# Pooled attention into a gated expert layer on one core: wider loads, block-by-block conversion of W's first half, and another order of the first loads

## The chip, the cores and the metric

One core of a Trainium2 chip runs the whole program. The metric is the device time of one execution in microseconds (us); for the kernel before it is 782.62 us, the median of three runs (781.56 to 783.02). The core's engines are called by the names of the profile: PE (matrix multiplies, with PEld for its weight loads), DVE (vector), ACT (scalar and activation functions), POOL (GpSimd) and SP (it only issues transfers here). Each engine works through its own list of instructions in the order in which the program emits them.

## The reference

```
q, k, v: 8 batches x 8 heads x 576 tokens x 64, float32
k_p, v_p = mean over groups of 8 tokens          # 72 pooled keys and values per head
scores   = q @ k_p^T / 8;  attn = softmax(scores)
x        = attn @ v_p, heads side by side        # 4608 tokens x 512
a, b     = x @ w1, x @ w2                        # 512 -> 1024 each
out      = ((a * b) @ w3) @ w_out                # 1024 -> 1024 -> 512, float32
```

The four weight matrices come as 64-bit floats, q, k and v as 32-bit ones.

## The kernel before, in words

There is nothing nonlinear between `w3` and `w_out`, so the kernel first forms W = w3 @ w_out (1024 x 512) and then needs only two products per token: into a and b, and with W. All products are done in three passes over a high and a low part of each operand (`PASSES`, high*high, high*low, low*high), which `split` (line 157) makes: ACT casts the high part, DVE subtracts it to get the low part.

**The first stage makes W's first half** (rows 0 to 511), in eight blocks `s` = 0 to 7. For each block two loads of 512 KB come in, `load_w3` (line 118) and `load_wo` (line 114). Each is a block of 64-bit floats that must be turned into 32-bit ones: `high` (line 131, ACT) takes the upper word, `low` (line 138, DVE) or `low_act` (line 143, ACT) takes bits of the lower word, and `conv_b` (line 152, DVE) joins them. The w3 block is then turned on PE by four transposes (`w_turn`, line 213), and both blocks are split. `w_block` (line 170) does this in three stages of a pipeline: its call `v` converts block v, turns and casts block v-1 and subtracts the low part of block v-2's second operand. `w_mm` (line 629) then adds 12 matrix products of 512 columns into four PSUM banks. So the turn of block 1 stands ahead of the products of block 0 on PE.

**The second stage makes W's second half** (s = 8 to 15), with `w_conv`, `w_conv2` and `w_split` (lines 220 to 227); the second operand stays in SBUF from the first stage. Beside it runs the attention of the first chunk of 384 tokens: keys of batch 0 are loaded (`load_k`, line 316: four loads, each with 72 partitions), summed in groups of eight (`prep_k`, line 325, on POOL by a tree of three adds, or on DVE by one reduction where `K_DVE` says so), transposed (`kt_mm`, line 335, four transposes of 72 columns into one PSUM bank) and scaled; queries are loaded (`load_q3`, line 292), transposed on PE and copied; then come scores, softmax (`soft1` to `soft3`, with the exponentials on ACT), the transposes of the probabilities and the product with the pooled values. The 72 keys of a head don't fit 128 partitions evenly for two heads, so 16 of the 144 rows of a pair of heads are handled apart: `load_vr` (line 360) loads them four times over, with a broadcast as the outermost dimension of the source.

**The third stage is the first chunk of the main loop** (m = 0): per block j of 128 hidden units `a_mm`, `b_mm` (12 products each) and, two steps later, `out_mm` (9 products), while the attention of the second chunk and the conversions of w1 and w2 (`load_w12`, line 125, `w12_conv`) run beside it. After it come ten more chunks in a steady loop and a short last piece.

**The order of the work is written by hand.** `at(kind, k, fn, ...)` (line 648) puts a step on a plan; the plan is sorted (line 777) by the whole part of k, then by kind (L loads, P work on DVE, ACT and POOL, with the turns of W, M matrix products, A products of the attention), then by the fraction of k. `F0` = 4, `K0` = 20 and `M0` = 36 are the steps at which the three stages begin. The order in which a step is emitted is the order in which every engine, SP among them, takes it up. A tile in SBUF or PSUM that has a limited number of buffers makes a load or a matrix product wait until an older user has let go: the raw w3 blocks use four cells in turn (`raw_cell(s % 4)`), keys and values four buffers (`st_tile`), attention's PSUM tiles (`patt`) three, and w1 and w2 go to cells in the order `FREED` (line 106), as W's products and conversions release them. SP waits at such a load, and every load behind it waits too.

`warm` (line 207) issues transposes that nobody reads, 36 at the very start and 12 before the first products of W.

## Time and profile before

| | before |
|---|---|
| median of 3 runs | 782.62 us (781.56 to 783.02) |
| profiled execution, its own time | 782.46 us |
| its span in the profile, first to last instruction | 780.7 us |
| PE busy | 756.3 us, 97% of the span |
| DVE, ACT, POOL busy | 60%, 37%, 25% |
| bytes read from and written to memory | 52.43 and 9.44 MB |

The span leaves 1.76 us of the execution's own time outside. The views used below are: the page (busy time by engine), the table by stage (busy time of each engine in a stretch of time, with the granted clock of PE as a share, the mean busy share of the 16 transfer engines and the rate of the transfers), the waits (who waited for whom, in total, how often, the longest), the timeline (start, length, engine, line, operation, out<-in, with the idle time ahead of it and what ended it in brackets) and the chain of work that ended last (start, length, engine, tile and line). "x12" is a count of instructions merged into one line. PE's records overlap, because products are pipelined: a group's pace is read from the starts of its neighbours.

### The profile page before, as it was taken

To read this page: it belongs to the slowest core of one execution; us is meant where nothing else is said; L and a number is where in the kernel's file an instruction comes from. 1 tells how busy PE (TensorE), PEld (TensorE's weight loads), DVE (VectorE), ACT (ScalarE), POOL (GpSimd) and SP (SyncE) were. 2 spreads that over 40 slices of the span, in tenths; PEclk is the share of its full clock that TensorE was granted. 3 is DMA by queue.
4 is the path that set the end of the run, shared out by engine and by line. 5 is a ranking of instruction groups with operands and counts; after the bars stand their busy time and mean duration, and the time that the engine had idled before them with its cause. 6 is when DMAs were issued, how large, how long until landed. Compare 5 with 4: busy or idle time off the path is not lost.

```text
span 780.7 us, 11495 instructions
## 1 busy us (share of the span) xinstructions
PE 756.3 (97%) x4146; PEld 699.9 (90%) x4146; DVE 468.1 (60%) x923; ACT 287.7 (37%) x710; POOL 195.2 (25%) x234
## 2 busy tenths in 40 slices
PE   8978989999999999999999999999999999999998
PEld 7767877999999998999999998999999989999997
DVE  6866887475484476485574576575574675662212
ACT  5567977332233333232233333322332332332211
POOL 2334565105208202006117202025035220000000
PEclk9999999999999999999999999999999999999999
DMA  9999970026245233037044323136154222120101
GB/s 329 280 210 212 271 169 15 1 78 126 55 116 107 62 99 66 7 111 146 23 122 87 94 69 61 41 89 128 41 134 96 70 68 46 53 50 1 40 1 41
DMA packets 123913, 74.43 MB, mean 95 GB/s; under 512 B 75600, under 2 KB 107600, under 8 KB 123856
## 3 DMA queue, kind: packets, MB, share of 16 engines
q1 hardware_dynamic: 123856, 73.69, 38.4%
q8 instruction: 33, 0.54, 0.3%
q14 instruction: 24, 0.20, 0.1%
HBM read 52.43 MB, written 9.44 MB: 79 GB/s over the span
## 4 chain that ended last, share of the span: by engine, by line
PE 76%; DVE 10%; DMA 5%; ACT 4%; SPq 2%; issue 1%; POOL 0%; POOLq 0%; DVEq 0%; ACTq 0%
PE o L609 22%; PE a L574 21%; PE b L574 21%; DMA raw<-in_moe_w_dram 4%; PE att L415 3%; PE o L635 2%; DVE T L498 2%; DMA st<-in_v_dram 1%; DVE E L453 1%; PE att L549 1%; PE att L551 1%; PE att L550 1%; PE att L548 1%; DVE E L433 1%; DVE mx L431 1%
## 5 line engine op out<-in xcount | busy, mean ns | idle before, releaser
L574 PE MATMUL a<-xT,hl 128*128 128x384 f32 x1152 | 221.0, 339 | 0.4 <-POOL hl L159 0.4
L574 PE MATMUL b<-xT,hl 128*128 128x384 f32 x1152 | 220.9, 339 | 0.0
L574 PEld LDWEIGHTS a<-xT,hl 128*128 128x128 f32 x1152 | 201.1, 188 | 5.4 <-POOL hl L159 0.7
L574 PEld LDWEIGHTS b<-xT,hl 128*128 128x128 f32 x1152 | 199.7, 188 | 0.0
L609 PE MATMUL o<-Wc,gh 128*128 128x512 f32 x576 | 180.6, 395 | 0.0
L373 POOL TENSOR_TENSOR st<-st 72x512 f32<-72x512 f32 (+1 forms) x53 | 71.8, 1354 | 225.6 <-DMA st<-in_k_dram 170.3
L609 PEld LDWEIGHTS o<-Wc,gh 128*128 128x128 f32 x576 | 106.7, 188 | 17.1
L594 DVE TENSOR_TENSOR a<-b,a 128x384 f32<-128x384 f32 x96 | 52.8, 550 | 111.5 <-PE b L574 111.5
L609 PE MATMUL o<-Wc,gl 128*128 128x512 f32 x288 | 114.3, 397 | 3.3 <-DVE gl L600 3.3
L595 ACT CAST gh<-a 128x384 fp32r<-128x384 f32 x96 | 49.3, 513 | 151.9 <-DVE a L594 151.9
L584 ACT COPY a<-a 128x384 f32<-128x384 f32 x96 | 45.9, 479 | 110.5 <-PE a L574 86.6
L436 ACT ACTIVATE E<-E 128x288 f32<-128x288 f32 (+1 forms) x70 | 31.1, 445 | 118.3 <-DVE E L433 118.3
L600 DVE TENSOR_TENSOR gl<-a,gh 128x384 fp32r<-128x384 f32 x96 | 63.6, 663 | 13.6 <-ACT gh L595 13.6
L609 PEld LDWEIGHTS o<-Wc,gl 128*128 128x128 f32 x288 | 54.1, 188 | 17.1 <-DVE gl L600 4.6
L560 DVE TENSOR_TENSOR xT<-att,xT 128x384 fp32r<-128x384 f32 x48 | 26.5, 555 | 60.7 <-ACT xT L559 60.7
L386 POOL TENSOR_TENSOR vbd<-vm,vbd 64x256 fp32r<-64x256 f32 x16 | 12.5, 781 | 183.7 <-ACT vbd L385 183.4
L415 PE MATMUL att<-kbd,qT 128*128 128x144 f32 (+1 forms) x320 | 52.3, 286 | 2.4 <-DVE PTx L532 2.2
L415 PEld LDWEIGHTS att<-kbd,qT 128*128 128x128 f32 (+1 forms) x320 | 47.2, 178 | 6.9 <-DVE PTx L532 2.9
L437 DVE TENSOR_REDUCE sm<-E 128x4 f32<-128x288 f32 (+1 forms) x70 | 31.6, 451 | 35.8 <-ACT E L436 35.8
L159 DVE TENSOR_TENSOR PTx<-PTx,PTh 128x512 fp32r<-128x512 f32 (+1 forms) x33 | 27.7, 838 | 35.0 <-ACT PTh L158 32.8
L374 POOL TENSOR_TENSOR st<-st 72x256 f32<-72x256 f32 (+1 forms) x53 | 44.5, 840 | 4.2
L431 DVE TENSOR_REDUCE mx<-att 128x4 f32<-128x288 f32 (+1 forms) x80 | 35.2, 440 | 14.9 <-PE att L415 14.9
(93 smaller groups left out, 802.5 us busy)
## 6 DMA issues: line engine op xcount, KB each, us to landing
raw<-in_moe_w_dram SPq DMA_DIRECT2D x32, 512.0 KB
PTx<-T SPq DMA_DIRECT2D x120, 96.0 KB
st<-in_k_dram SPq DMA_DIRECT2D x32, 288.0 KB
out_dram<-ob SPq DMA_DIRECT2D x35, 256.0 KB
st<-in_v_dram SPq DMA_DIRECT2D x32, 256.0 KB
qs<-in_q_dram SPq DMA_DIRECT2D x128, 48.0 KB
raw<-in_moe_w_out_dram SPq DMA_DIRECT2D x8, 512.0 KB
st<-in_v_dram SPq DMA_DIRECT2D x64, 64.0 KB
```

Of the source, the lines that this page charges most:

```text
L373: nc.gpsimd.tensor_tensor(out=t[:, :, 0:4], in0=t[:, :, 0:4], in1=t[:, :, 4:8], op=ALU.add)
L374: nc.gpsimd.tensor_tensor(out=t[:, :, 0:2], in0=t[:, :, 0:2], in1=t[:, :, 2:4], op=ALU.add)
L415: nc.tensor.matmul(out=ps[:nt, 2 * KP * j:2 * KP * (j + 1)], lhsT=qT[n][:, pr, off:off + nt], rhs=kbd[b % 2][:, pr], start=True, stop=True,)
L431: nc.vector.tensor_reduce(out=mx[:nt, hs], in_=sv, axis=AX.X, op=ALU.min)
L436: nc.scalar.activation(out=E[:nt, hs], in_=E[:nt, hs], func=AF.Exp, scale=-1.0)
L437: nc.vector.reduce_sum(out=sm[:nt, hs], in_=E[:nt, hs], axis=AX.X)
L574: nc.tensor.matmul(out=o, lhsT=w12[j, w][sw][:, kt * P:(kt + 1) * P], rhs=x[sx][:, kt], start=(i == 0), stop=(i == 3 * NK - 1))
L584: nc.scalar.copy(out=a, in_=gt[m, j][:, :CH])
L594: nc.vector.tensor_tensor(out=g, in0=ps[:, :CH], in1=g, op=ALU.mult)
L595: nc.scalar.copy(out=gh, in_=g)
L600: nc.vector.tensor_tensor(out=gl, in0=g, in1=f(gh), op=ALU.subtract)
L609: nc.tensor.matmul(out=oacc[m][t], lhsT=(gh, gl)[sg][:, c], rhs=W[j][sw], start=(j == 0 and i == 0), stop=(j == NJ - 1 and i == 2))
```

## The change

It does these things:

1. **Wide loads.** `load_k` takes the 576 pooled-key groups of a batch as rows of one list, 256 rows to a load on 128 partitions (two rows each) and a last load of 64: three loads for four. `load_v` takes 128 consecutive groups of a pair of heads in one load on 128 partitions: two for four. `load_vr` joins neighbouring rows, with the rows outermost and the broadcast inside: six loads for eight. `load_q3` loads two heads at once: four for eight in the first chunk, eight for sixteen in the second. The layouts that follow from it: sums of keys are written twice side by side (`dup`), so that one transpose gives both halves of the partitions, and `kt_mm` has six transposes in two PSUM tiles instead of four in one, `kt_post` four scalings instead of two. `K_DVE` keeps DVE reductions for the last load of 64 rows of batches 0 and 1 alone. The parts of `soft3` and `prep_vr` use the matching order.
2. **W's first half block by block.** `w_block(s)` converts block s, `w_block2(s)` turns and splits it, and then its products follow; no other block's turn stands ahead of them. For five of the eight blocks the lower word of the second operand is taken on ACT (`low_act`), not on DVE. In the first half the three passes run over both tiles together, with high*low last.
3. **Another order of the first loads.** All loads of W's first half go first, then w3's block 8, the keys and the queries of the first chunk, w3's blocks 9 and 10, the values, w3's block 11, the rows apart, and then the rest of w3.
4. **Second half converted later.** `w_conv`, `w_conv2` and `w_split` stand 2.5, 1.9 and 1 steps ahead of the products instead of 7, 6 and 1.5. The transposes of the first chunk's queries move from steps 17, 18, 19 and 20 to 19, 19, 20 and 20, the sums of its keys from 13.5 and later to 16 and later, those of its values from 22 to 24.
5. **At the start** 20 and 20 `warm` transposes for 36 and 12, the second lot behind the turn of block 0; half of the clearing of buffers goes from POOL to DVE, ahead of the mask.

```diff
+    WO_LOW_DVE = (0, 3, 6)
...
-    K_DVE = [(0, 3), (1, 1), (1, 3)]
+    K_DVE = [(0, 2), (1, 2)]
...
+    for i, eng in enumerate((nc.vector, nc.gpsimd)):
+        eng.memset(kbd[i], 0.0)
...
+    def w_block(s):
+        w_tiles(s)
+        r3, z3 = stage["w3", s]
+        ro, zo = stage["wo", s]
+        high(raw["w3", s], z3)
+        low(raw.pop(("w3", s)), r3)
+        high(raw["wo", s], zo)
+        if s not in WO_LOW_DVE:
+            low_act(raw["wo", s], ro)
+        conv_b(r3, z3)
+        if s in WO_LOW_DVE:
+            low(raw["wo", s], ro)
+        conv_b(ro, zo)
+
+    def w_block2(s):
+        ps, src = w_turn(s), f(stage["wo", s][0])
+        w3t[s], wo[s] = hl_cell(4 + s % 4), hl_cell(8 + s)
+        nc.scalar.copy(out=w3t[s][0], in_=ps)
+        nc.scalar.copy(out=wo[s][0], in_=src)
+        nc.vector.tensor_tensor(out=w3t[s][1], in0=ps, in1=f(w3t[s][0]), op=ALU.subtract)
+        nc.vector.tensor_tensor(out=wo[s][1], in0=src, in1=f(wo[s][0]), op=ALU.subtract)
...
+    def load_k(b, u):
+        t = stage["k", b, u] = st_tile([P, 2, POOL, D])
+        rows = k_in[b].rearrange("h (k e) d -> (h k) (e d)", e=POOL)
+        n = min(2 * P, H * KP - 2 * P * u)
+        p = min(P, n)
         nc.sync.dma_start(
-            out=t[:KP],
-            in_=k_in[b, 2 * pr:2 * pr + 2].rearrange("a (k e) d -> k a (e d)", e=POOL),
-        )
+            out=t[:p, :n // p].rearrange("p c e d -> p c (e d)"),
+            in_=rows[2 * P * u:2 * P * u + n].rearrange("(c p) x -> p c x", p=p))
...
+    KT = [(0, P, 0, 0), (1, P, 0, P), (2, P, 0, 2 * P), (3, P, 0, 3 * P), (3, P, 1, 0), (4, 64, 1, P)]
...
-                    out=t[32 * r:32 * r + 32, g],
-                    in_=src.unsqueeze(0).broadcast_to([4, KR, POOL * D]),
+                    out=t[32 * r:32 * (r + n), g].rearrange("p e d -> p (e d)"),
+                    in_=src[g].unsqueeze(1).broadcast_to([n * KR, 4, POOL * D]))
...
-        for it in its:
-            for i, (sa, sb) in enumerate(PASSES):
+        for i, (sa, sb) in enumerate(PASSES if h else PASSES[::2] + PASSES[1:2]):
+            for it in its:
...
-    at("L", F0 - 5, warm, 36)
-    at("M", F0 - 2, warm, 12)
-    for s in range(NJ + 2):
-        at("P", F0 + 2 * (s - 2), w_block, s)
+    at("L", F0 - 5, warm, 20)
+    at("M", F0 - 1, warm, 20)
+    for s in range(NJ):
+        at("P", F0 + 2 * (s - 1), w_block, s)
+        at("P", F0 + 2 * s - 1, w_block2, s)
...
-            at("L", k - 14, load_w3, s)
-            at("P", k - 7, w_conv, s)
-            at("P", k - 6, w_conv2, s)
-            at("P", k - 1.5, w_split, s)
+            at("L", {8: 7.1, 9: 7.4, 10: 7.5, 11: 7.7}.get(s, k - 10.4), load_w3, s)
+            at("P", k - 2.5, w_conv, s)
+            at("P", k - 1.9, w_conv2, s)
+            at("P", k - 1, w_split, s)
...
-    plan_k(0, K0 + 1, K0 - 13.5, K0 - 6.5, 1.5)
-    plan_q3(0, [K0 - 10.5 + 1.5 * pr for pr in range(NPR)], [K0 - 3, K0 - 2, K0 - 1, K0])
-    plan_v(0, K0 - 4.5, K0 + 5.5, K0 + 2, K0 + 11, K0 + 8.5)
+    plan_k(0, K0 + 1, [7.2] * 3, K0 - 4, 2)
+    plan_q3(0, [7.3] * NPR, [K0 - 1, K0 - 1, K0, K0])
+    plan_v(0, [7.6] * 2, 7.8, K0 + 4, K0 + 11, K0 + 8.5)
```

More of the change, by code (lines that the diff above doesn't have):

```diff
@@ L75 @@
     make_identity(nc, ident)
+    for i, eng in enumerate((nc.vector, nc.gpsimd)):
+        eng.memset(kbd[i], 0.0)
+        for s in range(2):
+            eng.memset(vbd[i][s].bitcast(F32), 0.0)
+        eng.memset(VR[i].bitcast(F32), 0.0)
     nc.vector.tensor_reduce(
         out=msk,
-        in_=ident.rearrange("p (a two e) -> p two a e", two=2, e=2 * KR),
+        in_=ident.rearrange("p (a two e) -> p two a e", two=2, e=2),
         axis=AX.XY,
@@ L295, in load_q3 @@
         for (b, s0, cnt, off) in pieces(n):
-            for par in range(2):
-                nc.sync.dma_start(
-                    out=stage["q", n][off // 3:(off + cnt) // 3, pr, :, par],
-                    in_=q[b, 2 * pr + par, s0:s0 + cnt, :].rearrange("(p i) d -> p i d", i=3))
+            nc.sync.dma_start(
+                out=stage["q", n][off // 3:(off + cnt) // 3, pr],
+                in_=q[b, 2 * pr:2 * pr + 2, s0:s0 + cnt, :].rearrange("a (p i) d -> p i a d", i=3))
     def q3_turn(n, pr):
@@ L335, in kt_mm @@
+    KT = [(0, P, 0, 0), (1, P, 0, P), (2, P, 0, 2 * P), (3, P, 0, 3 * P), (3, P, 1, 0), (4, 64, 1, P)]
     def kt_mm(b):
-        ps = patt.tile([P, 512], F32, tag="att", name="att")
-        kv = stage["kt", b] = ps[:, :NPR * KP].rearrange("p (a k) -> p a k", k=KP)
-        for pr in range(NPR):
+        kv = [patt.tile([P, 512], F32, tag="att", name="att") for _ in range(2)]
+        for c, p, x, o in KT:
             nc.tensor.transpose(
-                out=kv[:, pr], in_=km[b][:KP, pr].rearrange("k a d -> k (a d)"), identity=ident[:KP, :KP])
+                out=kv[x][:, o:o + p], in_=km[b][:p, c].rearrange("k a d -> k (a d)"), identity=ident[:p, :p])
+        stage["kt", b] = [kv[x][:, o:o + 2 * KP * a].rearrange("p (a h k) -> p a h k", h=2, k=KP)
+                          for x, a, o in ((0, 3, 0), (1, 1, 6 * KP - 3 * P))]
@@ L388, in prep_vr @@
     def prep_vr(b):
[L389 removed]
+        t = stage.pop(("vr", b))
+        m = t[:, :, 0]
         hi = p1.tile([P, 2, D], F32R, tag="vrh", name="vrh")
[L391 removed]
+        pool_tree(t, m)
         nc.scalar.copy(out=hi, in_=m)
@@ L677, in plan_k @@
     def plan_k(b, k, load, prep, d):
-        for pr in range(NPR):
-            at("L", load + 2 * pr, load_k, b, pr)
-            at("P", k - 1 if (b, pr) == (0, 3) else prep + d * pr, prep_k, b, pr)
+        for u in range(3):
+            at("L", load[u], load_k, b, u)
+            at("P", prep + d * u, prep_k, b, u)
         at("A", k, kt_mm, b)
```

119 lines of the change are left out of this document (37 added, 82 removed).

## The prediction

> **What bounds the kernel now.** I read the page first, then the table by stage, with cuts where W's first half, W's second half and the first main chunk end on PE, then PE's waits, and last the timelines of the first 32 us.
>
> ```profile
> PE 756.3 (97%) x4146; PEld 699.9 (90%) x4146; DVE 468.1 (60%) x923; ACT 287.7 (37%) x710; POOL 195.2 (25%) x234
> ```
> ```profile
> core 0 of [0], span 780.7 us
> core 0: us, PE busy (x) PEld busy (x) DVE busy (x) ACT busy (x) POOL busy (x), PEclk, DMA share, GB/s
> 0.00:42.40 42.40, 36.85 (x186) 30.46 (x186) 31.86 (x58) 23.34 (x39) 12.99 (x23) 0.96 1.00 298
> 42.40:86.20 43.80, 37.52 (x198) 30.91 (x198) 30.18 (x55) 33.60 (x105) 18.52 (x21) 0.96 0.92 216
> 86.20:143.70 57.50, 52.09 (x296) 46.72 (x297) 47.04 (x79) 41.49 (x115) 30.73 (x29) 1.00 0.52 120
> 143.70:776.80 633.10, 629.80 (x3468) 591.78 (x3467) 358.60 (x732) 188.90 (x452) 133.00 (x162) 1.00 0.30 71
> ```
>
> PE is the bound, and from 143.7 us on it is full (629.8 of 633.1). What can be won lies ahead of that: 5.55 us idle in the first stage (42.40 less 36.85), 6.28 in the second, 5.41 in the third; besides, PE's clock stood at 0.96 in the first two, which is 1.7 us lost in each (0.04 of 42.4 and of 43.8). And the first stage's busy time holds work that nobody needs:
>
> ```profile
> 1.36 6.20 PE L211 MATMUL att<-ident 128*128 128x128 f32 x36 [1.36 <-POOL ident masks.py:199]
> ...
> 11.39 0.63 PE L217 MATMUL att<-ident,Wc 128*128 128x128 f32 x4 [2.08 <-DVE Wc L154]
> 11.78 3.60 PE L635 MATMUL o<-hl 128*128 128x512 f32 x9
> ...
> 16.19 0.60 PE L217 MATMUL att<-ident,Wc 128*128 128x128 f32 x4
> ...
> 19.37 0.60 PE L217 MATMUL att<-ident,Wc 128*128 128x128 f32 x4
> ```
>
> Products of block 0 start at 11.78, right behind the turn of block 1 (11.39), which had waited for DVE. From turn to turn a block then takes 3.18 us (19.37 less 16.19) with PE full: eight blocks need 25.4, yet the stage took 30.6 from 11.78. The waits say where the rest went, in all stages:
>
> ```profile
> PE att L415 <- DVE PTx L532: 2.2, 1, 2.2
> PE att L217 <- DVE Wc L154: 2.1, 1, 2.1
> PE att L306 <- ACT Wc L158: 2.1, 1, 2.1
> PE o L635 <- DVE hl L188: 1.9, 2, 1.2
> PE att L217 <- ACT E L441: 1.9, 2, 1.3
> ```
>
> **First stage: block by block.** The timelines of ACT and DVE, with their waits in brackets:
>
> ```profile
> 6.30 0.70 ACT L136 ACTIVATE wt<-raw 128x512 f32<-128x512 f32 x1 [1.49 <-DMA raw<-in_moe_w_out_dram]
> 10.22 0.68 ACT L136 ACTIVATE wt<-raw 128x512 f32<-128x512 f32 x1 [0.50 <-DMA raw<-in_moe_w_out_dram]
> 13.58 0.58 ACT L196 CAST hl<-att 128x512 fp32r<-128x512 f32 x1
> 14.04 0.63 ACT L203 CAST hl<-wt 128x512 fp32r<-128x512 f32 x1
> 31.37 0.68 ACT L136 ACTIVATE wt<-raw 128x512 f32<-128x512 f32 x1 [1.36 <-DMA raw<-in_moe_w_out_dram]
> ```
> ```profile
> 4.13 1.30 DVE L141 TENSOR_SCALAR Wc<-raw 128x512 int32<-128x512 int32 x1 [2.31 <-DMA raw<-in_moe_w_dram]
> ...
> 15.48 0.68 DVE L188 TENSOR_TENSOR hl<-wt,hl 128x512 fp32r<-128x512 f32 x1
> 16.08 0.42 DVE L141 TENSOR_SCALAR wt<-raw 128x512 int32<-128x512 int32 x1
> 16.41 0.69 DVE L154 SCALAR_TENSOR_TENSOR Wc<-Wc 128x512 int32<-128x512 int32 x1
> ```
>
> Block 0's last piece lands at 6.30. High word 0.70, join 0.69, cast 0.63: its products can start at 8.3 instead of 11.8, since no other block's turn stands ahead. Block 1 lands at 10.22: high word 0.68, low word on ACT 0.68 (the same shape as the high word; its issue overlaps by 0.1), join 0.69, cast 0.63: products at 12.8. From then on the blocks are tied by a ring over three engines, because the new order keeps each engine in one block: DVE's subtraction (0.60 to the next start, 15.48 to 16.08), low word (0.33), join (0.69), PE's turn (0.60), two casts on ACT (0.46 to the next start, then 0.63): 3.31, with hand-overs about 3.4, against PE's own 3.18. The five extra low words on ACT lie beside this ring (ACT is busy 23.3 of 42.4). Six rings bring block 7 to 12.8 + 20.4 = 33.2, and its products end at 36.4. I add 0.8, half of the 1.7 us that the half-speed clock cost, since the change doesn't remove its cause for sure: 37.2 against 42.4, **-5.2 us**. Bounds: with PE as the only limit and no slow clock 35.1 (-7.3); with 3.7 a ring and all of the slow clock 39.9 (-2.5).
>
> The slow clock has a row of its own:
>
> ```profile
> 10.00:15.00 5.00, 3.61 (x13) 2.97 (x14) 4.19 (x9) 3.37 (x6) 0.00 (x0) 0.74 1.06 380
> ```
>
> The clock was down to 0.74 here, after 48 idle transposes and a gap of 2.08 us. The change leaves 20 at the start, which last until about 4.8 (20 of 36 in 6.20 us), and a gap until the turn of block 0 at about 5.5 (its w3 part is there at 4.13, then 0.70 and 0.69). The Trainium skill (TensorE: Matmul & The Clock Gate, Part 1) says that the clock falls after an idle window of some 3.4 us; by that the gap would be harmless and the 0.8 would go, 775.4 instead of the forecast. This trace doesn't agree fully, since a gap of 2.08 was enough here, so the 0.8 stays.
>
> Do the loads keep up? The last load of this half ended ACT's wait at 31.37. SP had held it back:
>
> ```profile
> 18.71 0.38 SPq L121 DMA_DIRECT2D raw<-in_moe_w_dram  x1
> ...
> 48.05 10.06 SPq L367 DMA_DIRECT2D st<-in_v_dram  x8
> ```
>
> The issue at 18.71 is block 8's, waiting for a raw cell that block 4's conversion frees, with block 7's two loads behind it. Now those two go ahead of it. 16 loads of 0.524 MB are 8.39 MB, and transfers ran at 298 GB/s or more over this stage: landed by 28.2 at the latest, 5 us ahead of the 33.2 where they are needed. Buffer clearing on DVE fits its idle 2.31 us ahead of 4.13; at worst it costs a few tenths, since 4.13 isn't where the chain is tied (6.30 is).
>
> **Second stage.** PE's needs stay the same (37.52 busy). What is new: behind the first half, DVE has W's four subtractions (a cast, 0.63, then 4 x 0.60), then the last keys' reduction, then the join of block 9 (0.69). The reductions of before:
>
> ```profile
> 93.36 2.02 DVE L330 TENSOR_REDUCE km<-st 72x128 f32<-72x1024 f32 x1
> ```
>
> The new one has half the elements a partition, about 1.0. That is 4.7 us until block 9 can be turned; PE has four turns of queries (0.33 each) and half of block 8's products (1.4, from 3.18 a block less the turn, halved) in front of that: 2.7. So PE waits about 2.0. The softmax of three tiles with exponentials on ACT and divisions on DVE interleaved as before leaves, by the order of the plan, another 2.6. Together 4.6 of idle time for 6.28; of the slow clock (1.7) I take half off: 1.7 + 0.9 = **-2.6 us**. Bounds: -8.0 if all idle time and slow clock go; upwards by the third rival.
>
> New waits at SP: the second load of values needs the buffer of the first keys, the rows apart that of the second keys (POOL's sums, ahead of everything else on POOL), and w3's block 11 a cell that block 7's conversion frees. Behind them stand w3's blocks 12 to 15. If the 3.0 MB from block 8 to block 9 (keys, queries and both blocks) move at no more than this stage's 216 GB/s, block 9 is there at 28.2 + 13.9 = 42.1, when PE is due to turn it. So even without faster transfers the wait is at most a us or so.
>
> **Third stage.** One of DVE's two reductions of 2.02 us becomes half as long and the other goes to POOL. DVE (47 of 57.5 busy) ended PE's longest wait there (2.2): **-1.0**, between 0 and the 5.4 of idle time.
>
> **Full stage.** Keys take six transposes of up to 128 columns instead of four of 72. From the chain of work, in the full stage and in the first:
>
> ```profile
> 604.83 0.25 PE att L339 x4
> ```
> ```profile
> 16.35 0.44 PE att L217 x4
> ...
> 53.67 3.80 ACT E L441 x23
> ```
>
> Four of 72 took 0.25, four of 128 took 0.44, 0.11 each. Six are 0.66, so 0.41 more in each of batches 2 to 7, where PE has no slack: **+2.5** (at 0.0625 each, the pace of the short ones, +0.8; with batches 0 and 1 as well +3.3). The second PSUM tile costs nothing there: the values' products of a chunk are two or more steps ahead. Strided parts of softmax, the additional scalings on ACT and POOL's longer last add lie under PE (DVE is busy 358.6 of 633.1, ACT 188.9).
>
> **Sum.** The profiled execution took 782.46 us, 1.76 more than its span and 0.16 below the median of 782.62. 782.46 - 5.2 - 2.6 - 1.0 + 2.5 = **776.2 us**; between 771 and 781 as the terms' bounds combine.
>
> **Rivals.**
>
> *All slack goes (chance 0.16).* The second stage loses all its idle time and slow clock (-8.0), the third 2.0: 782.46 - 5.2 - 8.0 - 2.0 + 2.5 = 769.8. For it: the biggest single waits have other orders now. Against it: softmax and the ring over three engines stay.
>
> *Transfers are the cap (0.11).* The engines for transfers are at a share of 1.00, 0.92 and 0.52, so a PE that is 8 us early may wait for w1 and w2 at the same time as before, and only the third stage's 1.0 and the 2.5 remain: 784.0. Against it: while the rows apart went out (10.06 us for 0.5 MB) the share fell by more than half,
>
> ```profile
> 55.00:60.00 5.00, 4.44 (x25) 3.66 (x25) 2.34 (x7) 3.88 (x24) 2.34 (x3) 1.00 0.43 148
> ```
>
> so there was room that the old shape of the loads left unused. The Trainium skill (DMA: Bandwidth & Descriptors, Why a DMA increments its semaphore by 16 and not by 1) gives a reason: a transfer uses the largest number of engines up to 16 that divides both outermost dimensions, so 12 of 16 for 72 partitions and 4 for a broadcast of four in front; after the change 16, and 8 or 16. The share of 0.43 agrees with that, and if it holds, this rival has less to stand on.
>
> *Late conversion, slower (0.07).* In the second half a block's conversion now stands 2.5 steps ahead. High word 0.70, join 0.69, turn 0.60, cast 0.63, subtraction 0.68 are 3.3 us in a row. A burst of exponentials (3.80) ahead of the first of them makes PE wait the full 3.3. If blocks 9 to 12 all do, PE waits 13.2 more: 782.46 - 5.2 + 13.2 - 1.0 + 2.5 = 792.0. It decides from about 10 us of idle time in the second stage (6.28 plus the 3.7 that the other terms bring). Against it: before, ACT's burst held the turns too (1.9 us in two waits), for want of PSUM tiles, with conversions long done.
>
> **Chances.** The forecast has 0.66. About 0.2% (1.6 us) is what a measurement of this kernel can tell from no change. Of the forecast's 0.66, 0.65 lie under 781.0; with the first rival 0.16 and 0.02 of the cap, faster has 0.83. Same has 0.05 (0.01, and 0.04 of the cap), slower 0.12 (0.05 of the cap, 0.07 late conversion). The range from 769.5 to 781.5 takes in the forecast's bounds and the first rival and leaves out some 0.17.
>
> **What would show it.** Products of block 0 at about 8.3 us and the end of the first half near 37; turns of the first half 3.2 to 3.5 us apart; no wait for a load of w_out after block 1; one wait of about 2 us on PE at the turn of block 9; W's second half ended near 78.5; six transposes of keys in about 0.66 us; the eight loads of 10 us become six in less than 5. The prediction is wrong if the first half ends later than 40, if the second stage has over 10 us of idle time on PE, or if the third stage is longer than 57.5.

## The result: slower, and the profile after

The changed kernel takes 791.37 us, the median of four runs (790.77 to 793.25), against 782.09 of the kernel before on the same chip: a ratio of 1.0131, 95% interval 1.0105 to 1.0156. The forecast was 776.2. The profiled execution took 790.98 us. Its page first, then the table by stage, cut at the same events as before (end of W's first half, of its second half, of the first main chunk on PE):

```profile
PE 760.4 (96%) x4154; PEld 698.4 (88%) x4154; DVE 465.9 (59%) x923; ACT 292.7 (37%) x731; POOL 171.5 (22%) x209
```
```profile
core 0: us, PE busy (x) PEld busy (x) DVE busy (x) ACT busy (x) POOL busy (x), PEclk, DMA share, GB/s
0.00:42.10 42.10, 35.30 (x172) 26.91 (x173) 31.82 (x52) 24.18 (x42) 10.90 (x18) 1.00 1.00 323
42.10:90.10 48.00, 38.89 (x207) 30.30 (x205) 29.41 (x59) 34.84 (x109) 17.03 (x21) 1.00 0.81 234
90.10:147.20 57.10, 52.40 (x298) 47.05 (x299) 47.56 (x81) 41.90 (x117) 29.57 (x28) 1.00 0.28 72
147.20:785.30 638.10, 633.66 (x3480) 594.15 (x3479) 356.54 (x732) 191.39 (x464) 113.97 (x144) 1.00 0.27 70
```

Against before the stages are 0.3 us shorter, 4.2 longer, 0.4 shorter and 5.0 longer. PE's clock stood at 1.00 throughout this execution (0.96 in the first two stages before), and still the first stage gained nearly nothing; its idle time is 6.8 us (42.10 less 35.30; 5.55 before). The second stage has 1.4 us more busy time and 2.8 more idle time. The last one, in which PE was full before, holds 3.9 us more of PE's work.

**First stage.** PE's timeline; a line of L201 is the turn of a block:

```profile
8.54 1.64 PE L629 MATMUL o<-hl 128*128 128x512 f32 x6
10.49 0.63 PE L201 MATMUL att<-ident,Wc 128*128 128x128 f32 x4 [0.31 <-DVE Wc L153]
10.87 0.48 PE L629 MATMUL o<-hl 128*128 128x512 f32 x1
...
12.33 1.64 PE L629 MATMUL o<-hl 128*128 128x512 f32 x6
...
14.34 0.63 PE L201 MATMUL att<-ident,Wc 128*128 128x128 f32 x4 [0.38 <-DVE Wc L153]
...
18.19 0.63 PE L201 MATMUL att<-ident,Wc 128*128 128x128 f32 x4 [0.37 <-DVE Wc L153]
...
36.42 0.63 PE L201 MATMUL att<-ident,Wc 128*128 128x128 f32 x4 [1.37 <-DVE Wc L153]
...
38.27 1.63 PE L629 MATMUL o<-hl 128*128 128x512 f32 x6
...
40.27 0.63 PE L201 MATMUL att<-ident,Wc 128*128 128x128 f32 x4 [0.37 <-DVE Wc L153]
```

The products of block 0 do start at 8.54, 3.2 us earlier than before. These six are half of them, though: the plan puts the turn of the next block between the two halves of a block's products, so that "no other block's turn stands ahead of them" holds for the first half alone. Block 0's other six products come from 10.87, behind the turn of block 1 at 10.49, and block 1's begin at 12.33. And a block takes 3.85 us (18.19 less 14.34), not 3.18, and each turn shown waits for DVE's joining step (L153). The ring can be read off the starts on ACT and DVE, for the block turned at 14.34:

```profile
15.00 0.59 ACT L186 CAST hl<-att 128x512 fp32r<-128x512 f32 x1 [1.05 <-PE att L201]
```
```profile
15.62 0.69 DVE L188 TENSOR_TENSOR hl<-att,hl 128x512 fp32r<-128x512 f32 x1 [0.82 <-ACT hl L186]
16.23 0.68 DVE L189 TENSOR_TENSOR hl<-wt,hl 128x512 fp32r<-128x512 f32 x1
16.83 0.42 DVE L140 TENSOR_SCALAR Wc<-raw 128x512 int32<-128x512 int32 x1
17.35 0.69 DVE L153 SCALAR_TENSOR_TENSOR Wc<-Wc 128x512 int32<-128x512 int32 x1
```

Turn to first cast 0.66, first cast to first subtraction 0.62, to the second subtraction 0.61, to the low part 0.60, to the join 0.52, join to the next turn (18.19) 0.84: 3.85 us. The second cast runs beside the first subtraction. Late in the stage two blocks take 4.80 and 5.72 us; there DVE runs beside POOL's sums over the keys:

```profile
28.92 1.63 DVE L153 SCALAR_TENSOR_TENSOR Wc<-Wc 128x512 int32<-128x512 int32 x1
30.48 0.95 DVE L140 TENSOR_SCALAR wt<-raw 128x512 int32<-128x512 int32 x1
```
```profile
28.73 1.27 POOL L363 TENSOR_TENSOR st<-st 128x512 f32<-128x512 f32 x1 [25.50 <-DMA st<-in_k_dram]
30.08 1.06 POOL L364 TENSOR_TENSOR st<-st 128x256 f32<-128x256 f32 x1
...
31.98 1.73 POOL L363 TENSOR_TENSOR st<-st 128x512 f32<-128x512 f32 x1
```

**Second stage.** PE's waits from 42 to 90 us:

```profile
PE att L201 <- DVE Wc L153: 3.5, 2, 2.0
PE att L469 <- DVE E L447: 1.7, 1, 1.7
PE att L201 <- DVE PTx L526: 1.5, 1, 1.5
PE att L409 <- DVE Wc L153: 1.1, 1, 1.1
```

3.5 of the 9.1 us idle are waits of two turns, those of blocks 9 and 14, for the joining step of a late conversion (first line). The fourth line, a wait of the scores, names that step too, but the same 1.1 us is put down to the exponentials in the run with the ring cut, and it stays where the conversions come earlier (both below): it is not counted here.

**Full stage.** PE around the key transposes of one batch, and PE's whole wait for the low half of g; the first two fences are after, the last two before:

```profile
553.15 2.25 PE L568 MATMUL a<-xT,hl 128*128 128x384 f32 x12
555.24 0.91 PE L331 MATMUL att<-ident,km 128*128 128x128 f32 x6
556.08 1.86 PE L568 MATMUL b<-xT,hl 128*128 128x384 f32 x9
```
```profile
PE o L603 <- DVE gl L594: 4.4, 3, 1.5
```
```profile
546.27 2.25 PE L574 MATMUL a<-xT,hl 128*128 128x384 f32 x12
548.36 0.42 PE L339 MATMUL att<-ident,km 72*128 72x72 f32 x4
548.58 2.33 PE L574 MATMUL b<-xT,hl 128*128 128x384 f32 x12
```
```profile
PE o L609 <- DVE gl L600: 3.3, 3, 1.2
```

From a's products to b's it is now 2.93 us instead of 2.31, 0.62 more in each of six batches, 3.7 together; the waits for g add 1.1.

### The profile page after: what moved, and what is told of

Same layout as the page of the kernel before. It is cut to its first block, busy times and chain, and to the rows that moved or that the text cites. A ratio compares the mean times of both kernels' runs of the same rounds, so it can differ in the third digit from the quotient of the medians.

```text
span 789.2 us, 11446 instructions
## 1 busy us (share of the span) xinstructions
PE 760.4 (96%) x4154; PEld 698.4 (88%) x4154; DVE 465.9 (59%) x923; ACT 292.7 (37%) x731; POOL 171.5 (22%) x209
## 4 chain that ended last, share of the span: by engine, by line
PE 73%; DVE 15%; ACT 7%; DMA 3%; issue 2%; SPq 0%; DVEq 0%; ACTq 0%
PE o L603 22%; PE b L568 21%; PE a L568 21%; PE att L409 3%; DVE T L492 2%; ACT E L435 1%; DVE E L447 1%; DMA PTx<-T 1%; DVE mx L425 1%; PE att L543 1%; PE att L545 1%; PE att L544 1%; PE att L542 1%; DVE Wc L153 1%; ACT E L430 1%
## 5 line engine op out<-in xcount | busy, mean ns | idle before, releaser
L363 POOL TENSOR_TENSOR st<-st 128x512 f32<-128x512 f32 (+1 forms) x46 | 59.9, 1303 | 225.4 <-DMA st<-in_k_dram 162.1
L594 DVE TENSOR_TENSOR gl<-a,gh 128x384 fp32r<-128x384 f32 x96 | 59.5, 620 | 13.6 <-ACT gh L589 13.6
L629 PE MATMUL o<-hl 128*128 128x512 f32 x144 | 45.7, 407 | 0.8 <-ACT hl L187 0.6
L158 DVE TENSOR_TENSOR PTx<-PTx,PTh 128x512 fp32r<-128x512 f32 (+1 forms) x33 | 25.8, 782 | 35.0 <-ACT PTh L157 31.7
```

Source lines behind the costliest of these rows:

```text
L363: nc.gpsimd.tensor_tensor(out=t[:, :, 0:4], in0=t[:, :, 0:4], in1=t[:, :, 4:8], op=ALU.add)
L594: nc.vector.tensor_tensor(out=gl, in0=g, in1=f(gh), op=ALU.subtract)
L629: nc.tensor.matmul(out=wacc[h][it], lhsT=w3t[s][sa][:, it * P:(it + 1) * P], rhs=wo[j][sb], start=(j == 0 and i == 0), stop=(j == NJ - 1 a ...
```

## The experiments

The table reads four marks off the timelines of the profiled executions, in us from the span's start: the first product of W's block 8, the first product into a, the last hidden block's first product into a of chunk 0 (from here PE is full), and the last copy of an output. The columns between them are stretches. Times and ratios come from the timed runs, the ratio against the kernel before on the same chip. Two things blur the first two columns. Up to block 8 "keys as before" has the changed kernel's code, and the marks still differ by 1.1 us (43.80 and 42.70). And in some profiles PE's granted clock stood at 0.50 for 3.4 us at a time, which costs up to 1.7 us where PE is full: ahead of block 8 once in before, rows as before, old pipeline and "ring cut, conversions earlier", twice in good parts and in good parts with conversions as before; between block 8 and a once in before, old pipeline, loads in old order, block 9's conversion later and its load first, twice in ring cut. The other profiles have none up to a. Differences smaller than that are not read.

| kernel | block 8 | to a | to a's last | to the last copy | last copy | median us | ratio (95%) |
|---|---|---|---|---|---|---|---|
| before | 45.12 | 41.88 | 56.74 | 633.54 | 777.28 | 782.09 | |
| changed | 42.70 | 48.33 | 56.19 | 638.74 | 785.96 | 791.37 | 1.0131 (1.0105–1.0156) |
| keys as before | 43.80 | 48.89 | 57.00 | 634.78 | 784.48 | 788.79 | 1.0101 (1.0084–1.0118) |
| rows as before | 44.54 | 48.99 | 55.85 | 637.31 | 786.69 | 790.36 | 1.0115 (1.0092–1.0139) |
| conversions earlier | 42.12 | 44.55 | 56.09 | 638.68 | 781.44 | 786.44 | 1.0071 (1.0056–1.0086) |
| ring cut | 39.82 | 50.79 | 56.19 | 638.57 | 785.37 | 788.09 | 1.0099 (1.0077–1.0120) |
| no key sums | 39.77 | 48.25 | 56.16 | 638.81 | 782.99 | 788.53 | 1.0103 (1.0083–1.0123) |
| old pipeline | 39.35 | 48.72 | 56.10 | 638.60 | 782.77 | 786.85 | 1.0077 (1.0059–1.0094) |
| ring cut, conversions earlier | 41.93 | 43.77 | 56.15 | 638.63 | 780.47 | 785.55 | 1.0059 (1.0040–1.0077) |
| loads in old order | 42.06 | 50.39 | 56.14 | 638.74 | 787.33 | 793.70 | 1.0160 (1.0135–1.0185) |
| four costs undone | 40.65 | 45.55 | 56.72 | 633.41 | 776.34 | 781.66 | 1.0010 (0.9996–1.0025) |
| good parts | 43.43 | 43.76 | 55.81 | 633.38 | 776.38 | 781.70 | 0.9999 (0.9982–1.0017) |
| good parts, conversions as before | 47.47 | 41.64 | 55.87 | 633.40 | 778.37 | 782.28 | 1.0008 (0.9992–1.0025) |
| block 9's conversion later | 39.76 | 47.20 | 55.93 | 633.42 | 776.32 | 780.90 | 0.9980 (0.9964–0.9997) |
| block 9's load first | 38.33 | 48.16 | 55.88 | 633.44 | 775.80 | 780.44 | 0.9993 (0.9977–1.0009) |
| repeated rows later | 38.22 | 45.05 | 55.84 | 633.38 | 772.48 | 777.99 | 0.9952 (0.9934–0.9970) |

**Keys as before** (batches 1 to 7: loads, sums and transposes of before):

```diff
+        if b > 0:                                  # load_k; prep_k, kt_mm and kt_post alike
+            t = stage["k", b, u] = st_tile([P, 2, POOL, D])
+            nc.sync.dma_start(
+                out=t[:KP], in_=k_in[b, 2 * u:2 * u + 2].rearrange("a (k e) d -> k a (e d)", e=POOL))
+            return
...
-        for u in range(3):
+        for u in range(4 if b else 3):
```

> The changed kernel with the keys of batches 1 to 7 loaded, summed and turned as before (four loads of 72 rows, four transposes of 72x72 in one bank, two copies); batch 0, the values and everything else as changed. Theory: of the 5.2 us that the full stage lost, 3.7 are the six key transposes (2.93 us between the products around them instead of 2.31, in six batches). Then the stage from 147.2 to the last output falls from 638.1 to about 634.4 us, the gap around the key transposes is 2.3 us again, and the kernel takes about 787.5 us; the three waits of output products for the low half of g stay at 1.5 us each. Rival: the transposes only show where time is lost to something common to the whole stage (values' and keys' loads in other shapes, less work on POOL); then the stage stays within 1 us of 638.

The full stage is 634.78, 3.96 shorter, and the waits for g stay at 4.4: the theory's size and its sign. The time, 788.79, is 1.3 above the forecast; block 8 starts 1.1 later. The third stretch grows by 0.8, so batch 1's keys are better in the new form.

**Rows as before** (`soft3`, `load_vr`):

```diff
-            nc.scalar.copy(out=R[:nt, :, :, :, dup, 0], in_=er)
+            nc.scalar.copy(out=R[:nt, :, :, dup, 0], in_=er)
```

> The changed kernel with the pooled values' repeated rows in the order of before: the probabilities of the remaining keys are written in runs of 8 instead of with a stride of four elements, and their values are loaded in eight pieces instead of six. Theory: the strided writes cost VectorE 0.054 and ScalarE 0.061 us an instruction, and through them three products of the output a chunk with a key batch wait 0.35 us longer; the full stage falls by 1.0 to 1.3 us, to 637.5 (from the last chunk-0 product of a to the last copy; 638.7 as changed), the waits of the output products for the low half of g from 4.4 to about 3.3 us; 790 us in all. Rival: these waits come with the key transposes, and the layout costs nothing: the stage stays at 638.5 to 639 us, the waits at 4.4.

The full stage falls by 1.43, and the waits for g to

```profile
PE o L603 <- DVE gl L594: 3.1, 3, 1.0
```

So the new order of the rows costs 1.4 us there: by the profile a strided subtraction of 128x64 takes DVE 274 ns instead of 221, a cast ACT 306 instead of 245. With the keys' 4.0 that is the whole of what the full stage lost (5.2).

**Conversions of W's second half earlier:**

```diff
-            at("P", k - 2.5, w_conv, s)
-            at("P", k - 1.9, w_conv2, s)
+            at("P", k - (2.5 if s == NJ else 4.5), w_conv, s)
+            at("P", k - (1.9 if s == NJ else 3.9), w_conv2, s)
```

> The changed kernel with the conversions of blocks 9 to 15 planned one block (two steps) earlier, block 8's as changed. Theory: the second stage lost 4.2 us against before, of which 1.4 are transposes of queries and keys that now fall into it and 2.8 are idle time, from the conversions that stand two and a half steps ahead of their turn, behind the softmax on ACT and VectorE. Then the waits of the turns and of the scores for the second conversion step (3.5 us in two waits and 1.1 in one) are gone, those for the softmax's own outputs stay or grow by up to 1 us, and the second stage falls from 48.0 to 44.5 to 46 us; the first stage grows by at most 0.7, as block 9's conversion now falls into it; 788 to 789 us in all. Rival: ACT and VectorE are simply full in this stage (29 and 35 us of 48 and more around the softmax), so that the waits move to the softmax's outputs: 47.5 to 48.5 us for the stage, 790.5 to 791.5 in all.

The stretch from block 8 to a falls from 48.33 to 44.55. PE's waits there, the first three lines:

```profile
PE att L469 <- DVE E L447: 1.7, 1, 1.7
PE att L409 <- DVE Wc L153: 1.1, 1, 1.1
PE att L201 <- DVE PTx L526: 1.0, 1, 1.0
```

The two waits of turns for L153 (3.5) are gone from the list, those for the softmax's outputs stay: the theory's case. The wait of the scores (1.1) stayed, which it had also called gone, and the time, 786.44, is 1.6 under its range.

**Ring cut** (w3's block s+1 converted ahead of block s's casts and subtractions):

```diff
-        at("P", F0 + 2 * (s - 1), w_block, s)
+        at("P", F0 + 2 * (s - 1) - (1.5 if s else 0), w_block_a, s)  # high, low, conv_b of w3
+        at("P", F0 + 2 * (s - 1), w_block, s)                        # those of w_out
```

> The changed kernel with the work of a block of the first half split in two: high part, low part and joining of w3's block s+1 are issued before the casts and subtractions of block s, so that the turn of s+1 no longer waits for them; the same instructions otherwise. Theory: the turns come 3.86 us apart because turn, cast, two subtractions, the low part and the joining follow one another in a ring over three engines. Cut, the period is VectorE's own work for a block (0.52 + 0.69 + 0.69 + 0.60 + 0.60 = 3.1 us, 3.5 with the low part of w_out): turns 3.1 to 3.5 us apart, the products of block 8 start at 38 to 39.5 instead of 42.1, and the kernel takes about 788 us. Rival: the loads or VectorE's rate are the bound, and the turns stay 3.7 to 3.9 us apart: 791 us.

```profile
15.07 0.60 PE L203 MATMUL att<-ident,Wc 128*128 128x128 f32 x4
...
18.36 0.60 PE L203 MATMUL att<-ident,Wc 128*128 128x128 f32 x4
```

The period is 3.29 us, and block 8's products start at 39.82 (38 to 39.5 was expected), although block 0's now start at 10.28: ACT's first step for block 1, which waited 2.14 us for its load, stands ahead of block 0's casts. The ring was the bound, and the time, 788.09, is the one expected. The next stretch is 50.79 in this profile, 2.5 longer than as changed. Two turns now wait 4.5 us for their late conversions instead of 3.5; right behind the longer of these waits (2.48 us, until 45.03) the clock fell, and again from about 75.5 us, up to 3.4 us lost in all. The row of the table by stage around the first of these falls (clock third from the end):

```profile
45.00:50.00 5.00, 4.97 (x19) 4.01 (x20) 1.72 (x3) 3.12 (x7) 3.99 (x5) 0.66 0.56 158
```

So it is not shown that the second stage gave anything back, as the next expectation supposes. The profiled execution took 790.40, 2.3 more than the median. **Both edits:**

> Both earlier edits at once: the ring of the first half cut (39.8 us instead of 42.7 until the products of block 8, of which the second stage gave 2.5 back, 50.8 instead of 48.3) and the conversions of blocks 9 to 15 one block earlier (second stage 44.6 alone). Theory: what gave the ring's gain back was the late conversions, bound by VectorE and ScalarE; an earlier start alone just waits for them. With both, the second stage takes 45 to 46.5 us and the two gains add: 784 to 785.5 us in all. Rival: the second stage ends by something the two edits don't touch (the late loads of the last blocks and of w1 and w2, which end at the same time whatever starts earlier): the stage stays at 47 us or more and the kernel at 786.4, the time with the earlier conversions alone.

43.77 us for that stretch, less than forecast, and 785.55 us. Block 8 starts 2.1 later than with the ring cut alone (41.93). Block 7's turn comes 0.6 later (38.03 for 37.40); block 9's conversion now falls into the first half, and ACT waits 1.8 us there for that block's load. The other 1.5 lie where the clock stood at 0.50, from 38.8 to 42.2. By the ratios the two edits gain 0.32% and 0.60%, together 0.72%, each with 0.2% or more of uncertainty: whether they add in full can't be told.

**No key sums:**

```diff
-            pool_tree(t, m, dup=2)
+            if b == 0:
+                nc.gpsimd.tensor_copy(out=m, in_=t[:, :, 0].unsqueeze(2).broadcast_to([p, n // p, 2, D]))
+                return
+            pool_tree(t, m, dup=2)
```

> The changed kernel without the sums over the keys of batch 0 on GpSimd (it copies the first of the eight rows instead, one instruction for three; this leaves out that part of the computation). Theory: blocks 6 and 7 of the first half take 4.8 and 5.7 us instead of 3.86 because VectorE's instructions are slower while GpSimd sums keys (the joining step 1.63 and 1.0 us instead of 0.69). Without the sums they take 3.9 to 4.2, and the first stage ends 2 to 2.8 us earlier, at 39.3 to 40.1 us; the kernel takes 788 to 789 us. Rival: the loads of queries and keys that land at that time slow VectorE, or the joining of block 6 waits for its data: blocks 6 and 7 stay at 4.8 and 5.7 us, 790.5 to 791.5 us in all.

The two blocks take 3.85 and 4.06 us; block 8 starts 2.93 us earlier. DVE's joining steps at the place where one took 1.63:

```profile
28.59 0.69 DVE L153 SCALAR_TENSOR_TENSOR Wc<-Wc 128x512 int32<-128x512 int32 x1
```

In those two blocks POOL's sums cost 2.6 us (4.80 and 5.72 before). In the kernel before two blocks took 4.62 us each for 3.19, 2.9 in all. There DVE also waited 1.29 us for a load in the first of them, so how much of it was POOL's is not shown; but slow blocks at this place are not what the change brought.

**Old pipeline** in W's first half (`w_block` of before), the rest as changed:

```diff
-    for s in range(NJ):
-        at("P", F0 + 2 * (s - 1), w_block, s)
-        at("P", F0 + 2 * s - 1, w_block2, s)
+    for s in range(NJ + 2):
+        at("P", F0 + 2 * (s - 2), w_block, s)
```

> The changed kernel with before's three-stage pipeline in W's first half (the turn of a block stands two steps ahead of its products, its casts and subtractions spread over the next block); loads, startup, keys, values and the second half as changed. Theory: block by block the turns come 3.86 us apart, in the old pipeline 3.19, but the old one starts its first products some 3 us later (11.78 against 8.54); over eight blocks the two cancel. Then the turns here come 3.2 us apart (4.6 at the two blocks under the key sums), the first products start at 10.5 to 11.8 us, and the products of block 8 start within 1.5 us of the changed kernel's 42.7; 790 to 792 us in all. Rival: the first half is bound by the loads, or by VectorE's sum of work in either form: turns 3.7 us apart and more, and the products of block 8 at 44.5 or later.

```profile
22.05 0.60 PE L216 MATMUL att<-ident,Wc 128*128 128x128 f32 x4
...
25.24 0.60 PE L216 MATMUL att<-ident,Wc 128*128 128x128 f32 x4
```

3.19 us a block, first products at 11.22, both as expected; but the two do not cancel. Block 8 starts at 39.35, 3.35 earlier than block by block, and the last copy is 3.2 earlier. The old form has the next block's turn done ahead; PE, not the ring, is its bound. Block by block was the wrong half of the change's trade.

**Loads in old order**, wide forms kept:

```diff
-            at("L", {8: 7.1, 9: 7.4, 10: 7.5, 11: 7.7}.get(s, k - 10.4), load_w3, s)
+            at("L", k - 10.4, load_w3, s)
...
-    plan_k(0, K0 + 1, [7.2] * 3, K0 - 4, 2)
-    plan_q3(0, [7.3] * NPR, [K0 - 1, K0 - 1, K0, K0])
-    plan_v(0, [7.6] * 2, 7.8, K0 + 4, K0 + 11, K0 + 8.5)
+    plan_k(0, K0 + 1, [K0 - 13.5, K0 - 11.5, K0 - 9.5], K0 - 4, 2)
+    plan_q3(0, [K0 - 10.5 + 1.5 * pr for pr in range(NPR)], [K0 - 1, K0 - 1, K0, K0])
+    plan_v(0, [K0 - 4.5, K0 - 3.5], K0 + 5.5, K0 + 4, K0 + 11, K0 + 8.5)
```

> The changed kernel with its loads in about the order of before: keys and queries of the first chunk between the blocks of W, the values after them, the wide forms kept; conversions and everything else as changed. Theory: the order of the loads has little part in the loss: the waits in both halves are for conversions, not transfers. The products of block 8 start within 1.5 us of 42.7 (the key sums of GpSimd lie over other blocks), the first product of a within 1.5 us of 91.0, 790 to 792.5 us in all. Rival: the late loads of w3's last blocks and of w1 and w2, behind the values, hold the second half up, and the old order wins 2 us or more: 789 or less.

The stretches agree with the theory (42.06, and a at 92.44); the time, 793.7, is 1.2 above its range. The new order is no part of the loss. Whether it gains anything can't be told: a comes 1.4 us later without it, but up to 1.7 were lost to the clock on the way, and the intervals of the ratios overlap.

**Four costs undone:** the first four edits together, the ring cut only from block 2 on (`s > 1` for `s`).

> The changed kernel with the four found costs undone: ring cut from block 2 on (so that the first product isn't held), conversions one block earlier, keys of batches 1 to 7 and the repeated rows as before. Left of the change: blocks one by one in the first half, wide loads of queries, values and of batch 0's keys, the order of the loads, the start. Theory: the terms add: products of block 8 at 38 to 39.5 us, second stage 44.5 to 46, third 56.2, full stage 633.5 to 634; 777 to 780 us in all, 2 to 4 us under the kernel before. Rival: they overlap in the second stage (same cover on VectorE and ScalarE), which takes 47 or more: 781 us or more.

**Good parts:** the old pipeline, conversions earlier, rows as before, and keys as before from batch 2 on (`b > 1` for `b > 0`).

> The parts of the change that proved good, alone: wide loads of queries and values, the new order of the loads, the start, and the new keys of batches 0 and 1. As before: the three-stage pipeline of W's first half, the keys of batches 2 to 7, the order of the repeated rows. The conversions of blocks 9 to 15 stand one block earlier than in the changed kernel. Theory: the terms add: products of block 8 at 39.4 to 41 us, second stage 43.8 to 45.5, third 56.2, full stage 633.4; last copy at 773 to 776 (777.3 before), 1.5 to 4 us under the kernel before. Rival: VectorE, full in the old pipeline (3.1 of 3.19 us a block), can't take block 9's conversion as well, and the first half gives back what the second gains: last copy at 777 or later, no faster than before.

And the same with the **conversions as before:**

```diff
-            at("P", k - (2.5 if s == NJ else 4.5), w_conv, s)
-            at("P", k - (1.9 if s == NJ else 3.9), w_conv2, s)
-            at("P", k - 1, w_split, s)
+            at("P", k - 7, w_conv, s)
+            at("P", k - 6, w_conv2, s)
+            at("P", k - 1.5, w_split, s)
```

> The same kernel with the second half's conversions planned as in the kernel before, three and a half blocks ahead of the products. Theory: what limits the second stage is only that a conversion comes before the softmax that would hold it up; three and a half blocks ahead put three blocks' conversions into the first half, where VectorE has 0.1 us to spare in 3.19: the first half takes 42 to 44 us and the second 41.5 to 43, together within 1 us of the run with one block ahead. Rival: idle time under the loads at the start takes them in, and both stages together are 2 us or more shorter than with one block ahead.

The full stage comes to 633.4 in all three, but the times, 781.7 to 782.3, can't be told from before: the gains that were forecast did not come. The first, 781.66, has its rival's time without its rival's mark (45.55, not 47 or more); block 8 comes at 40.65 instead of 38 to 39.5. In the second of them block 8 starts 4.1 us later than with the old pipeline alone. DVE's timeline there (L187 is block 7's last subtraction):

```profile
36.70 0.50 DVE L140 TENSOR_SCALAR Wc<-raw 128x512 int32<-128x512 int32 x1 [4.02 <-DMA raw<-in_moe_w_dram]
37.13 0.68 DVE L187 TENSOR_TENSOR hl<-wt,hl 128x512 fp32r<-128x512 f32 x1
```

Block 9's conversion waits for its load, which the new order puts behind the queries, and the first half's last subtraction stands behind it on DVE; PE waits 3.2 us for that. Behind this wait the clock stood at 0.50 for 6.8 us, up to 3.4 lost (old pipeline alone: 1.7 ahead of block 8). A row of the table by stage from there:

```profile
40.00:45.00 5.00, 5.00 (x18) 4.11 (x18) 4.41 (x7) 4.50 (x8) 3.78 (x4) 0.62 0.64 232
```

With conversions as early as before it is worse, a at 89.11 where within 1 us of 87.19 was expected: ACT waits 12.6 us for loads of w3 there, and DVE 6.7.

**Block 9's conversion later**, then **its load first**, then **the repeated rows later:**

```diff
-            at("P", k - (2.5 if s == NJ else 4.5), w_conv, s)
+            at("P", k - {8: 2.5, 9: 3.8}.get(s, 4.5), w_conv, s)
...
-            at("L", {8: 7.1, 9: 7.4, 10: 7.5, 11: 7.7}.get(s, k - 10.4), load_w3, s)
+            at("L", {8: 7.1, 9: 7.25, 10: 7.5, 11: 7.7}.get(s, k - 10.4), load_w3, s)
...
-    plan_v(0, [7.6] * 2, 7.8, K0 + 4, K0 + 11, K0 + 8.5)
+    plan_v(0, [7.6] * 2, K0 - 2.2, K0 + 4, K0 + 11, K0 + 8.5)
```

> The combined kernel once more (old three-stage pipeline, old keys from batch 2 on, old order of the repeated rows, wide loads, new load order and start), with only block 9's conversion moved behind the last subtractions of the first half, and those of blocks 10 to 15 one block early. Theory: what the first combined run gave back was VectorE's wait of 4.02 us for the load of block 9, with the low part of block 7's w_out queued behind it and PE waiting 3.2 us for that. Behind those subtractions the same wait holds up nobody: products of block 8 at 39.4 to 41 us, first product of a at 84 to 86 instead of 87.2, last copy at 773 to 775 (777.3 before): 778.5 to 780 us, 1.5 to 3 under the kernel before. Rival: block 9's load is the bound itself, and the time that the first half gains is lost at turn 9: first product of a at 86.7 or later, and no difference from the kernel before.

> The combined kernel of the run before, with one line changed: block 9's load is issued between the keys and the queries of the first chunk instead of behind the queries. Theory: in the run before ScalarE stood 5.72 and VectorE 2.53 us waiting for that load, with the casts of block 8 and of W's first half behind them in their queues, and so the second stage took 47.2 instead of the 44 to 45 us that earlier conversions give. With the load before the queries both waits are under 1 us, products of block 8 start at 38 to 39.8 us, the first product of a at 83.5 to 85.2 instead of 86.96, and the kernel takes 778 to 779.5 us. Rival: it isn't the load but the queue of casts and subtractions of W's first half, the keys' sum on VectorE and the queries' turns that all fall between blocks 8 and 10; the first product of a stays at 86 or later, and the queries, now later, add a wait of their own: 780.5 to 782.

> The combined kernel of the run before, with one line changed again: the eight loads of the repeated rows' values are issued behind block 12's load instead of ahead of it. In the run before the wait for block 9's load was gone, but the first product of a still came at 86.48: ScalarE now stood 2.43 us waiting for block 12's load, which is issued at 43.8 behind those eight (7.35 us on the queue), and the exponentials of chunk 0 stood behind that wait; PE waited 3.14 us for them. Theory: the loads of W's second half, each held by the ones put ahead of it, are what holds the second stage now. With block 12's load first the wait is under 0.5 us, PE's for the exponentials 1.1 as in the changed kernel, and the first product of a comes at 83.8 to 85.3: 777.5 to 779.5 us. Rival: the wait moves on once more, to the later loads or to the repeated rows themselves, and the first product of a stays at 85.9 or later.

ACT's rows for the first step of a conversion in the three, in this order: block 9's in each, and block 12's below it in the second and third:

```profile
38.57 0.67 ACT L135 ACTIVATE Wc<-raw 128x512 f32<-128x512 f32 x1 [5.72 <-DMA raw<-in_moe_w_dram]
```
```profile
33.29 0.66 ACT L135 ACTIVATE Wc<-raw 128x512 f32<-128x512 f32 x1 [0.86 <-DMA raw<-in_moe_w_dram]
...
50.73 0.67 ACT L135 ACTIVATE Wc<-raw 128x512 f32<-128x512 f32 x1 [2.43 <-DMA raw<-in_moe_w_dram]
```
```profile
33.37 0.68 ACT L135 ACTIVATE Wc<-raw 128x512 f32<-128x512 f32 x1 [0.76 <-DMA raw<-in_moe_w_dram]
...
47.74 0.67 ACT L135 ACTIVATE Wc<-raw 128x512 f32<-128x512 f32 x1
```

In the first, block 8 came early (39.76) and a at 86.96 all the same, the rival's mark, with ACT's wait of 5.72 for block 9's load. But the clock stood at 0.50 from about 43 to 46.5; without the 1.7 that this can cost, a lies in the theory's range, so this profile does not decide between them. With the load moved ahead, that wait shrank to 0.86 and another came (2.43, block 12's load), with chunk 0's exponentials behind it: PE waited 3.14 us for them, and the clock fell once more. a came at 86.48, the rival's mark, though not for the reason it gave. With the eight loads moved behind block 12's, block 12's wait is gone, PE waits 1.1 at that place, and the clock stays at 1.00: a at 83.26, 777.99 us, 0.48% under the kernel before (0.30 to 0.66%). So the order of the loads did hold the stage; how much of the 3.2 us between the last two is the wait, and how much the clock that fell behind it, these profiles don't separate. This version beats both kernels.

## Why the prediction was wrong

The forecast was 14.8 us short of the profiled execution's 790.98: 4.9 in the first stage, 6.8 in the second, 0.6 in the third, 2.5 in the full one.

- **First stage (-5.2 forecast, -0.3 came).** The start was right (products of the first two blocks at 8.3 and 12.8; 8.54 and 12.33 came). What failed is "tied by a ring ... about 3.4" us. The ring was the right mechanism, cut by an experiment, but mis-sized, 3.85. I led it through "two casts on ACT" (0.46 and 0.63) and one subtraction; it goes through the first cast and both subtractions (0.62 and 0.61). I took the low part's 0.33 to the next start, as in rows where the next step didn't need its result; the join does, and starts 0.52 later. Likewise I counted join to turn as 0.69 (0.84) and turn to cast as 0.60 (0.66). Over six rings that is 2.7 us. Left out were POOL's sums (2.8 in this profile, 2.6 by the experiment) and the turn that stands between the two halves of a block's products: block 7, begun at 38.27, ends at 42.1, 3.8 us later, where I counted 3.2. The 0.8 of slow clock wasn't there. -0.47 + 2.73 + 2.81 + 0.63 - 0.80 = 4.90. The larger mistake: the 5.2 us between 25.4 and 30.6 were to be won by taking the old pipeline apart, though it held PE full; with it the first half is 3.4 us shorter than block by block.
- **Second stage (-2.6 forecast, +4.2 came).** 4.5 of the 6.8 between them is idle time (9.1 for 4.6). The wait of 2.0 at block 9 came (1.56), but "as before leaves, by the order of the plan, another 2.6" failed: 7.5 came. The rival "late conversion" was in it, with 0.07: block 14's turn, too, waits 1.95 for its conversion, and moving the conversions earlier gives 3.8 back. As recorded the rival had blocks 9 to 12 each wait 3.3, 13.2 together; the two waits are 3.5. Its 792.0 is close to 791.4 by luck: the first stage's missing gain and the full stage made up for the rest. The other 2.3 is busy time, 1.4 more where 0.9 less was forecast: "PE's needs stay the same" failed. As the clock stood at 1.00 where before had lost up to 1.7 us, the work itself grew by as much as 3.1. 18 transposes of queries instead of 12 and six of keys instead of four are part of it; the rest is not traced here.
- **Third (-1.0; -0.4).** Batch 1's keys in their new form are worth 0.8 there by the experiment, and the strided rows take some 0.3 of it back (56.19 against 55.85).
- **Full stage (+2.5; +5.0).** Right in kind: six transposes cost. The size was off: I counted the transposes' own time, 0.41 more; between the products it is 0.62. And "strided parts of softmax ... lie under PE" failed: 1.4 us by the experiment, because in three places products wait on DVE for g, and there instructions longer by 0.05 make PE's work late.
- **Transfers.** The wide loads did what they should (the eight loads of 10.06 us take 5.3 as six), and nothing waited for a load of w_out after block 1; that PE would gain by it did not follow.

## What to carry to other kernels

Before a software pipeline is flattened, follow one item's steps around the engines by start-to-start times of steps that need each other's results: if that ring is longer than the busiest engine's work for an item, the pipeline's depth was paying for itself. A conversion moved closer to its use needs the free time of every engine it passes, and on an in-order queue a conversion that waits for a load holds up all behind it, so an earlier plan and the order of loads have to be moved together. Where the bound engine is full, 0.6 us of extra work for it in a small preparation step is multiplied by the batches, and 0.05 us on a neighbour's steps counts wherever it waits for them. And before a stretch of one profile is compared with that of another, the granted clock of both has to be looked at: half a clock for 3.4 us was as large here as many of the differences.

## What the runs showed of the hardware

POOL's sums lengthen some of DVE's instructions and not others: a join of two SBUF tensors took 1.63 us for 0.69, its end 0.55 behind POOL's, while a subtraction with one operand in PSUM kept its time in the same stretch:

```profile
32.49 0.68 DVE L188 TENSOR_TENSOR hl<-att,hl 128x512 fp32r<-128x512 f32 x1
33.26 1.01 DVE L189 TENSOR_TENSOR hl<-wt,hl 128x512 fp32r<-128x512 f32 x1
```

The Trainium skill (SBUF — State Buffer, SBUF: two separate sides) describes this as an exclusive lock on ports that DVE and GpSimd share, held for a whole instruction and taken by DVE instructions with two SBUF inputs, among others. This trace agrees: lengthened are those with two inputs in SBUF (1.63 and 1.01, by 0.94 and 0.33, where 1.08 and 0.45 were left of POOL's instruction). The low part, with one such input, is lengthened too (0.95 for 0.42); whether that falls under the "others", no run here shows. A longer sum on POOL is thus not free under DVE.

The weight load of the last, 64-row transpose of a batch's keys starts 0.17 us late, waiting for nothing that the profile shows; the five of 128 rows ahead of it have no such gap:

```profile
555.06 0.64 PEld L331 LDWEIGHTS att<-ident,km 128*128 128x128 f32 x5
555.87 0.14 PEld L331 LDWEIGHTS att<-ident,km 64*128 64x128 f32 x1 [0.17 <-issue]
```

PE's clock falls in pieces of one length: wherever it fell up to a, in ten of the sixteen profiles, the granted clock was 0.50 for 3.4 us (in good parts for 6.8). It did not follow the length of the gap ahead. With 2.22 us of gap after the warm transposes (old pipeline) it stood at 0.66 from 10 to 15 us, with 2.33 (repeated rows later) at 1.00; it fell behind a gap of 1.37 (rows as before, at 37 us) and not behind one of 2.09 (four costs undone, at 38 us). What decides it stays open. The Trainium skill (TensorE: Matmul & The Clock Gate, Part 1) has the clock follow a free-running window of about 3.4 us, by which a gap's place would count beside its length. The length of the pieces agrees with that; but all these gaps (and the 2.08 in the kernel before) are shorter than the idle window it asks for.
